# 38 more products on one tile of a fused attention and expert kernel

## The chip, the cores and the metric

The kernel runs on one core of a Trainium2 chip. The metric is the device time of one execution in microseconds. TensorE (PE) multiplies matrices, its weight loads are shown as PEld; VectorE (DVE), ScalarE (ACT) and GpSimd (POOL) work element by element, and SyncE (SP) issues most DMA transfers.

## The reference

Windowed causal attention over 8 batches, 8 heads, 576 positions and 64 channels per head, with a window of 64, followed by a gated expert layer (RMS norm, two products to 1536 columns, silu of one times the other, one product back to 512) over the 4608 tokens.

```python
scores = scale * np.matmul(q, k.transpose(0, 1, 3, 2))
mask = (rel >= 0) & (rel < window)
scores = np.where(mask, scores, -1000000000.0)
attn = np.exp(scores - np.max(scores, axis=-1, keepdims=True))
attn = attn / (np.sum(attn, axis=-1, keepdims=True) + 1e-09)
attn_out = np.matmul(attn, v)
x = np.ascontiguousarray(attn_out.transpose(0, 2, 1, 3)).reshape(B * S, H * D)
rms = np.sqrt(np.mean(x * x, axis=-1, keepdims=True) + 1e-06)
xn = x / rms * rms_g
g = xn @ w_gate
silu = g * (1.0 / (1.0 + np.exp(-g)))
val = xn @ w_val
out = silu * val @ w_out
```

The queries and keys are some four times larger than the draw that the reference's attention starts from, and the weights come as double precision.

## The kernel before, in words

Two heads make a pair; a batch has four pairs, so there are 32, and pair 4 is the first of the second batch. The expert layer takes the tokens in tiles of 512. The first batch's attention, the loading of the first weights and the first token tile are interleaved by hand: the program's steps are recorded, and then emitted in the order of the table ORDER. Each entry of it is an engine (t TensorE, v VectorE, s ScalarE, g GpSimd), the name of the tile that the step writes, and a count. Every engine takes its own steps in that order. Recorded steps are all listed under line 214, or 184 once recording is over.

The names that matter here:

- **ssq** holds the sums of squares of the first batch's attention output; tot adds them over partitions. VectorE then finds the inverse roots of the 576 means by a seed and three Newton steps, in ssq again.
- **rb** is the spread: four float32 products that copy the roots to all partitions (each shows as two passes in the profile).
- **xb** is the attention output, scaled by rb and the norm's weights; **xn** its two half-precision parts, high by ScalarE, low by GpSimd; **pv** and **pg** are the expert layer's first products, from xn.
- **mp** and **mn** are powers of two taken from the bytes of a double-precision weight, **pw** (bf16 products with a unit matrix) brings them together, and VectorE makes the float32 weight **wt** of it.
- **sc** are scores of a pair, **p** the masked scores, whose row minimum goes to st.
- **warm** are products of a constant with itself, which nothing reads. They are recorded as 24 tiles of up to 40 products; the table emits as many as it names.

TensorE writes into PSUM, which has eight banks. The pool ps_mi has one bank, and each tile that is taken from it is placed there:

```python
ps_mi = early.enter_context(tc.tile_pool(name="ps_mi", bufs=1, space=PSUM))
t = ps_mi.tile([P, TT], F32, tag="mi", name=f"warm_{k}")
n2 = ps_mi.tile([P, TT], F32, tag="mi", name=f"n2_{c}")[:, :2]
t = ps_mi.tile([P, TT], F32, tag="mi", name=f"sc_{n}_{g}_{h}")
```

The last of these is the scores of the second head of a pair from the second batch on (scores, line 630); the first head's are in ps_sc. VectorE reads the scores in the step masked. A tile framework adds the waits between engines, from what each instruction reads and writes and from which tiles share a place.

Of the kernel before, what the change touches and what calls it, by code (L numbers as in the profile page):

```python
# [90 lines left out]
g.ssq_0 s.mn_0_1 v.wt3 t.warm_1*2 t.tr_3_1_1*2 t.xp_3_0*6 v.top_0 t.xp_3_0*2 s.st_0_2 t.xp_3_0*2 t.pw_0_1_0 s.pt_3_1_1  # L91
t.pw_0_1_0 s.xb_0 s.kv_5 g.ssq_0 v.wt4 t.warm_1*2 t.xp_3_1*8 v.top_0 t.pw_0_1_1 s.xb_0 t.pw_0_1_1 s.kv_3 s.mp_1_1
v.sq_0 v.ssq_0 t.warm_1*3 t.n2_0 v.z_0 v.wt4 t.warm_2*2 t.tot_0*3 s.mn_1_1 t.tot_0 t.sc_4_0*3 v.ws_0 t.sc_4_0*2 v.wt3
t.sc_4_0 s.st_1_2 t.sc_4_0*4 s.kv_5 t.pw_1_1_0 v.ws_0 v.ssq_0 t.pw_1_1_0 v.ssq_0*2 s.mp_0_2 v.ssq_0*2 v.p_4_0_0
v.ssq_0*2 s.wt1 v.ssq_0*4 v.wt5 s.mn_0_2 t.rb_0_0 g.wt1 t.rb_0_0 v.p_4_0_1 t.rb_0_0 v.p_4_0_0 t.rb_0_0 v.p_4_0_0
t.pw_0_2_0 v.p_4_0_1 s.wt0 v.p_4_0_0 t.pw_0_2_0 v.xb_0 t.sc_4_1*2 v.wt6 t.sc_4_1 s.xn_0 t.sc_4_1*5 v.xb_0 t.pw_1_1_1
g.xn_0 t.pw_1_1_1 v.p_4_1_1 s.xn_0 v.xb_0 t.pv_0_0 s.mn_1_2 t.pv_0_0 g.xn_0 v.p_4_1_0 t.pv_0_0 v.wt5 t.pv_0_0 v.wt0
# [1428 lines left out]
```

## Time and profile before

| | us |
|---|---|
| Median of 3 runs (955.16 to 956.2) | 955.55 |
| The profiled execution | 954.38 |
| Its span, first to last instruction | 952.4 |
| TensorE busy | 931.9 |
| VectorE busy | 625.4 |
| ScalarE busy | 510.9 |
| GpSimd busy | 495.6 |

The page gives busy time by engine and in 40 slices, the chain of work that ended last, and groups of instructions by line, operation and tile. Beside it the trace answers for stretches of time (busy time of each engine, granted TensorE clock, DMA) and lists the instructions of an engine in order of time: start, length, engine, line, operation, output and inputs, count, and in brackets how long the engine sat idle before it and who ended that. The length of a TensorE product includes its way through the array, so products that follow each other overlap, and the distance of their starts is what one costs. The mean granted clock over the span is 0.996.

### The profile page before, as it was taken

How to read it: one execution, taken by the hardware profiler on the slowest of the kernel's cores; microseconds unless marked ns; L12 is line 12 of the kernel's file. 1: busy time of each engine (PE TensorE's matmuls, PEld its weight loads, DVE VectorE, ACT ScalarE, POOL GpSimd, SP SyncE). 2: the span in 40 equal slices, each digit the busy share in tenths (PEclk: the TensorE clock that was granted, in tenths of full speed). 3: DMA queues.
4: the chain of work that ended last, by engine and by line, in shares of the span. 5: the costliest groups of instructions: out<-in, count | busy, mean ns of one | idle time of the engine just before them, and what ended most of it. 6: DMA issues, size and time to landing. Idle time of an engine off the chain costs nothing.

```text
span 952.4 us, 20830 instructions
## 1 busy us (share of the span) xinstructions
PE 931.9 (98%) x7860; PEld 610.0 (64%) x7860; DVE 625.4 (66%) x1721; ACT 510.9 (54%) x1303; POOL 495.6 (52%) x634
## 2 busy tenths in 40 slices
PE   7699999999999999999999999999999999999998
PEld 5455454444454444788478856885688568848865
DVE  6888879778886876576757665776676555513540
ACT  7778985454444453566456645664465335413430
POOL 4355444978575783677466747764777122200210
PEclk9899999999999999999999999999999999999999
DMA  7655752515424661467245733564355226614300
GB/s 280 225 167 180 238 177 76 154 38 161 131 82 135 205 198 69 149 217 259 86 139 200 251 122 120 184 245 163 88 195 182 93 72 190 218 45 133 112 12 34
DMA packets 81316, 143.44 MB, mean 151 GB/s; under 512 B 25792, under 2 KB 38336, under 8 KB 81216
## 3 DMA queue, kind: packets, MB, share of 16 engines
q1 hardware_dynamic: 80640, 140.93, 45.4%
q8 instruction: 62, 1.02, 0.5%
q10 hardware_dynamic: 576, 1.18, 0.3%
q14 instruction: 38, 0.31, 0.1%
HBM read 121.64 MB, written 20.45 MB: 149 GB/s over the span
## 4 chain that ended last, share of the span: by engine, by line
PE 90%; DVE 3%; ACT 2%; POOL 2%; issue 1%; POOLq 0%; DVEq 0%; ACTq 0%
PE bk L184 51%; PE po L184 10%; PE pv L184 7%; PE pg L184 7%; PE xp L184 3%; PE pg L214 3%; PE pv L214 3%; PE sc L184 2%; POOL pm L184 1%; PE rb L184 1%; PE pw L214 1%; PE xp L214 1%; DVE ssq L214 1%; DVE th L184 1%; POOL h L184 0%
## 5 line engine op out<-in xcount | busy, mean ns | idle before, releaser
L184 PEld LDWEIGHTS <-wt 128*128 128x128 f16 x3624 | 353.2, 98 | 109.6 <-issue 4.6
L184 POOL TENSOR_TENSOR pm<-pm,st 32x288 f32<-32x288 f32 (+1 forms) x384 | 266.0, 693 | 62.4 <-DVE st L184 15.4
L184 PEld LDWEIGHTS <-h 128*128 128x128 f16 x1308 | 126.6, 98 | 142.3 <-issue 3.9
L184 PE MATMUL bk<-xn,wt 128*128 128x256 f16 x1728 | 207.3, 273 | 0.6 <-DVE u L184 0.5
L184 PE MATMUL bk<-wt,h 128*128 128x512 f16 (+1 forms) x900 | 191.1, 371 | 0.0
L184 POOL TENSOR_TENSOR h<-th,h 128x512 f16<-128x512 f32 x78 | 93.6, 1201 | 170.2 <-ACT h L184 156.2
L184 PE MATMUL bk<-wt,wt 128*128 128x256 f16 x1224 | 150.4, 273 | 0.3 <-ACT u L184 0.3
L184 ACT ACTIVATE pm<-pm,st 128x128 f32<-128x128 f32 (+1 forms) x216 | 83.9, 389 | 37.8 <-DVE st L184 36.7
L184 PE MATMUL po<-wt,h 128*128 128x512 f16 x408 | 90.9, 379 | 0.7 <-DVE wt L214 0.7
L184 ACT CAST h<-th 128x512 f16<-128x512 f32 x94 | 58.0, 617 | 51.7 <-DVE th L184 51.6
L184 POOL TENSOR_TENSOR xn<-xb,xn 128x448 f16<-128x448 f32 (+7 forms) x45 | 38.4, 861 | 83.5 <-ACT xn L184 81.1
L184 DVE SCALAR_TENSOR_TENSOR th<-th,bk 128x256 f32<-128x256 f32 x108 | 44.8, 415 | 49.6 <-ACT th L184 49.5
L184 ACT ACTIVATE th<-bk,hsc 128x256 f32<-128x256 f32 x108 | 48.0, 472 | 46.9 <-DVE bk L184 28.7
L184 DVE TENSOR_TENSOR bk<-bk,s 128x512 f32<-128x512 f32 x36 | 25.1, 696 | 69.2 <-PE bk L184 42.2
L184 PE MATMUL pv<-xn,wt 128*128 128x512 f16 x288 | 66.5, 379 | 0.0
L184 PE MATMUL pg<-xn,wt 128*128 128x512 f16 x288 | 66.1, 379 | 0.0
L184 ACT ACTIVATE ot<-bk,hsc 128x512 f32<-128x512 f32 (+1 forms) x25 | 16.8, 670 | 62.8 <-PE bk L184 62.8
L184 DVE CUSTOM_DVE_ANT_0 pm<-sc,blocked 128x128 f32<-128x128 f32 x191 | 48.7, 282 | 0.0
L184 DVE SCALAR_TENSOR_TENSOR th<-bk,th 128x256 f32<-128x256 f32 x108 | 45.8, 424 | 3.7
L214 PEld LDWEIGHTS <-wt 128*128 128x128 f16 x288 | 27.9, 99 | 31.6 <-issue 1.3
L184 ACT CAST xn<-xb 128x448 f16<-128x448 f32 (+7 forms) x56 | 23.8, 430 | 39.9 <-DVE xb L184 39.8
L184 DVE STREAM_TRANSPOSE pm<-pm 128x512 f32<-128x512 f32 (+1 forms) x72 | 39.6, 554 | 7.9 <-POOL pm L184 7.9
(179 smaller groups left out, 1318.2 us busy)
## 6 DMA issues: line engine op xcount, KB each, us to landing
wt<-sevens SPq DMA_DIRECT2D x108, 512.0 KB, 4.9
kv<-kv SPq DMA_DIRECT2D x28, 608.0 KB, 4.7
wt<-sevens SPq DMA_DIRECT2D x36, 256.0 KB, 3.1
q<-q SPq DMA_DIRECT2D x28, 288.0 KB, 3.7
kv<-kv SPq DMA_DIRECT2D x56, 128.0 KB, 5.0
out<-ot SPq DMA_DIRECT2D x27, 256.0 KB, 2.1
st<-w_gate SPq DMA_DIRECT2D x6, 1024.0 KB, 5.5
st<-w_val SPq DMA_DIRECT2D x6, 1024.0 KB, 5.3
```

What stands on the lines that cost most here:

```text
L184: return real(*args, **kw)
L214: steps[name].popleft()()
```

## The change

One entry is added to the table ORDER: 38 products of tile warm_3, each 128 by 128 by 256 columns in bf16.

```diff
-t.sc_4_0 s.st_1_2 t.sc_4_0*4 s.kv_5 t.pw_1_1_0 v.ws_0 v.ssq_0 t.pw_1_1_0 v.ssq_0*2 s.mp_0_2 v.ssq_0*2 v.p_4_0_0
+t.sc_4_0 s.st_1_2 t.sc_4_0*4 s.kv_5 t.pw_1_1_0 v.ws_0 v.ssq_0 t.pw_1_1_0 t.warm_3*38 v.ssq_0*2 s.mp_0_2 v.ssq_0*2 v.p_4_0_0
 v.ssq_0*2 s.wt1 v.ssq_0*4 v.wt5 s.mn_0_2 t.rb_0_0 g.wt1 t.rb_0_0 v.p_4_0_1 t.rb_0_0 v.p_4_0_0 t.rb_0_0 v.p_4_0_0
```

The products are those of keep_warm:

```python
for k in range(WARM[1]):
    t = ps_mi.tile([P, TT], F32, tag="mi", name=f"warm_{k}")
    for _ in range(WARM[0]):
        nc.tensor.matmul(t[:, :WC], lhsT=bright.to_broadcast([P, P]), rhs=bright.to_broadcast([P, WC]), start=True, stop=True)
```

On TensorE, before, from the last scores of pair 4's first half to the spread of the roots (the number behind a name is the buffer's, and in brackets stand the engines whose counters an instruction waits for):

```order
L214 MATMUL sc_4_0_1_270<-kv_4_265,q_4_264 64x64
L214 LDWEIGHTS unit_106 [waits DVE_49]
L214 MATMUL pw_1_1_0_276<-mp_1_1_274,unit_106 128x512 [waits Activation_49]
L214 LDWEIGHTS unit_106
L214 MATMUL pw_1_1_0_276<-mn_1_1_275,unit_106 128x512 [waits Activation_49]
L214 MATMUL rb_0_0_260<-ssq_0_185,first_of_108 128x144 [waits DVE_49,PE_49]
L214 MATMUL rb_0_0_260<-ssq_0_185,first_of_108 128x144 x2
L214 MATMUL rb_0_0_260<-ssq_0_185,first_of_108 128x80
```

The same place in the changed kernel, the first two of the 38 pairs and what follows the last:

```order
L214 MATMUL pw_1_1_0_276<-mn_1_1_275,unit_106 128x512 [waits Activation_49]
L214 LDWEIGHTS one_107 [waits DVE_49]
L214 MATMUL warm_3_137<-one_107 128x256 [waits PE_49]
L214 LDWEIGHTS one_107
L214 MATMUL warm_3_137<-one_107 128x256
...
L214 MATMUL rb_0_0_260<-ssq_0_185,first_of_108 128x144 x3
L214 MATMUL rb_0_0_260<-ssq_0_185,first_of_108 128x80
L214 LDWEIGHTS unit_106
```

Before, rb waited until VectorE's counter stood at 123, which its last Newton step sets. Now the first weight load of the block waits until it stands at 129, and rb has no wait of its own. On VectorE the rows of this place are the same in both kernels. The counter reaches 129 with the last row but one shown here, the read of the fifth mask:

```order
L214 SCALAR_TENSOR_TENSOR wt5_86<-st_1_1_259,pw_1_1_0_276 128x512 [waits DMAHW3_49,PE_49]
L214 ISA p_4_0_1_272,st_4_0_273<-sc_4_0_1_270,blocked_111 128x128
L214 ISA st_4_0_273 128x1
L214 ISA p_4_0_0_271,st_4_0_273<-sc_4_0_0_269,blocked_111 128x128
...
L214 ISA p_4_0_0_271,st_4_0_273<-sc_4_0_1_270,blocked_111 64x64
L214 ISA st_4_0_273 64x1
L214 SCALAR_TENSOR_TENSOR xb_0_184<-xb_0_184,gsb_114,rb_0_0_260 128x512 [waits PE_49]
```

Nothing moved on VectorE; TensorE's rb now stands behind the block.

## The prediction

> **What bounds the kernel now.** I read the page's head first, then the chain of waits, then the stretches of 2 us around the place of the change, and last the instructions of each engine there.
>
> ```profile
> span 952.4 us, 20830 instructions
> PE 931.9 (98%) x7860; PEld 610.0 (64%) x7860; DVE 625.4 (66%) x1721; ACT 510.9 (54%) x1303; POOL 495.6 (52%) x634
> PE 90%; DVE 3%; ACT 2%; POOL 2%; issue 1%; POOLq 0%; DVEq 0%; ACTq 0%
> 52.00:952.40 900.40, 894.82 (x7423) 586.06 (x7421) 584.44 (x1537) 472.32 (x1192) 473.25 (x595) 1.00 0.45 146
> ```
>
> TensorE is busy for 98% of the span and carries 90% of the chain that ended last. From 52 us to the end (the last row) it lacks 5.58 us of being busy throughout, at full clock (1.00). So whatever moves TensorE's work at 52 us moves the end by about as much. The change stands ahead of that point, in a stretch where TensorE does wait:
>
> ```profile
> core 0: us, PE busy (x) PEld busy (x) DVE busy (x) ACT busy (x) POOL busy (x), PEclk, DMA share, GB/s
> 38.00:40.00 2.00, 1.65 (x31) 0.85 (x30) 1.86 (x8) 2.00 (x2) 0.00 (x0) 1.00 0.98 306
> 40.00:42.00 2.00, 0.00 (x0) 0.00 (x0) 1.90 (x7) 2.00 (x3) 0.85 (x1) 0.95 0.89 329
> 42.00:44.00 2.00, 0.00 (x0) 0.00 (x0) 1.93 (x3) 1.23 (x2) 1.41 (x1) 0.50 0.61 220
> 44.00:46.00 2.00, 1.25 (x5) 1.29 (x6) 1.95 (x12) 0.00 (x0) 0.00 (x0) 0.50 0.00 0
> 46.00:48.00 2.00, 2.00 (x15) 1.16 (x17) 1.20 (x4) 0.31 (x1) 0.00 (x0) 0.50 0.01 4
> 48.00:50.00 2.00, 1.93 (x21) 0.88 (x14) 2.00 (x6) 1.17 (x3) 1.33 (x2) 0.84 0.00 0
> ```
>
> TensorE does nothing from 40 to 44 us, its granted clock (PEclk) falls to 0.50, and it is back at 1.00 only after 48 us. Finer stretches place both edges:
>
> ```profile
> 41.60:41.80 0.20, 0.00 (x0) 0.00 (x0) 0.20 (x1) 0.20 (x1) 0.20 (x1) 1.00 1.05 410
> 41.80:42.00 0.20, 0.00 (x0) 0.00 (x0) 0.20 (x1) 0.20 (x1) 0.20 (x1) 0.51 1.05 410
> 48.40:48.60 0.20, 0.20 (x8) 0.00 (x0) 0.20 (x2) 0.00 (x0) 0.20 (x1) 0.50 0.00 0
> 48.60:48.80 0.20, 0.20 (x5) 0.10 (x2) 0.20 (x1) 0.00 (x0) 0.20 (x1) 0.92 0.00 0
> ```
>
> The clock closes at 41.80. It opens at 48.63, because 0.92 is the mean of 0.03 us at 0.50 and 0.17 at 1.00. The instructions of TensorE in this stretch, and a few rows of the same view from elsewhere that price them (columns: start, length, engine, line, operation, out<-in, count; in brackets the idle time before and who ended it; the first row is the summary by tile, with the shortest, median and longest of 31 products in ns):
>
> ```profile
> L214 PE MATMUL warm<-one x31: 269/285/421, 0.9 to 37.8; 128*128 128x256 bf16 x31
> 0.90 3.17 PE L214 MATMUL warm<-one 128*128 128x256 bf16 x14 [0.90 <-DVE one L214]
> 6.36 0.62 PE L214 MATMUL warm<-one 128*128 128x256 bf16 x4
> 37.65 0.38 PE L214 MATMUL warm<-one 128*128 128x256 bf16 x2 [0.50 <-DVE z L214]
> 39.27 0.38 PE L214 MATMUL pw<-mn,unit 128*128 128x512 bf16 x1
> 44.74 2.12 PE L214 MATMUL rb<-ssq,first_of 128*128 128x144 f32 x8 [5.10 <-DVE ssq L214]
> 46.66 0.63 PE L214 MATMUL pw<-mp,unit 128*128 128x512 bf16 x1
> 47.09 0.63 PE L214 MATMUL pw<-mn,unit 128*128 128x512 bf16 x1
> 48.70 0.39 PE L214 MATMUL pw<-mp,unit 128*128 128x512 bf16 x1
> 48.93 0.38 PE L214 MATMUL pw<-mn,unit 128*128 128x512 bf16 x1
> 51.05 0.59 PE L214 MATMUL pv<-xn,wt 128*128 128x512 f16 x2 [0.65 <-POOL xn L214]
> 156.76 1.03 PE L184 MATMUL rb<-ssq,first_of 128*128 128x144 f32 x8
> ```
>
> TensorE's last work before the gap ends at 39.27 + 0.38 = 39.65. It then waits 5.10 us for VectorE's roots (ssq) and runs the spread, rb, at half clock in 2.12 us. What VectorE does meanwhile decides this case:
>
> ```profile
> 37.44 0.15 DVE L214 TENSOR_SCALAR z<-n 128x2 int32<-128x2 int32 x1
> 43.95 0.65 DVE L214 SCALAR_TENSOR_TENSOR ssq<-ssq 128x144 f32<-128x144 f32 x2
> 45.12 0.28 DVE L214 CUSTOM_DVE_ANT_0 p<-sc,blocked 128x128 f32<-128x128 f32 x1
> 46.13 0.08 DVE L214 DVE_READ_ACCUMULATOR2_ANT st<- 64x1 f32 x1
> 46.91 0.75 DVE L214 SCALAR_TENSOR_TENSOR xb<-xb,gsb,rb 128x512 f32<-128x512 f32 x1 [0.69 <-PE rb L214]
> 47.76 0.69 DVE L214 SCALAR_TENSOR_TENSOR wt<-st,pw 128x512 int32<-128x512 int32 x1
> 48.36 0.74 DVE L214 SCALAR_TENSOR_TENSOR xb<-xb,gsb,rb 128x512 f32<-128x512 f32 x1
> 49.14 0.62 ACT L214 CAST xn<-xb 128x512 f16<-128x512 f32 x1 [0.83 <-DVE xb L214]
> 49.83 1.17 POOL L214 TENSOR_TENSOR xn<-xb,xn 128x512 f16<-128x512 f32 x1 [0.29 <-ACT xn L214]
> ```
>
> The roots are ready at 44.60. From 45.12 to 46.21 VectorE masks the scores of pair 4, waiting for nothing, and then waits 0.69 us for rb. From there the stretch is a relay: xb, ScalarE's xn, GpSimd's xn, and TensorE's pv at 51.05.
>
> **The change part by part.** It adds 38 weight loads and 38 products on TensorE between pw_1_1_0 and rb_0_0, and nothing elsewhere. The order of VectorE, ScalarE, GpSimd and SyncE around it is the same. If the block could start at 39.65 it would fill the gap. But it can't: its output tile, warm_3, is in the only bank of pool ps_mi, and so is the tile sc_4_0_1, which TensorE has just written. The first weight load of the block carries a wait on VectorE, and the counter value in the built program is the one that the last mask read of pair 4 sets, the row that ends at 46.13 + 0.08 = 46.21. The trace has the like of it in small: the two warm products at 37.65 sat 0.50 us until VectorE had read n2, which lies in that bank (z in the row). So the block leaves the gap empty, and rb, which was free to start at 44.74, now queues behind 38 products that begin after 46.21. TensorE takes its work in the written order, so everything after rb queues too, and VectorE's xb, ScalarE's and GpSimd's xn with it. The masks themselves need only what TensorE wrote before 39.65, so there is no lock, and they stay where they are.
>
> *Start.* The wait on z ended at 37.44 + 0.15 and the products began 0.06 us later; rb began 0.14 us after the roots. I take 0.10: the block starts at 46.31.
>
> *Price of one product.* At half clock two pw products of 512 columns start 0.43 us apart (46.66, 47.09), so 0.215 us for 256 columns; at full clock 0.23 us (48.70, 48.93), so 0.11. The warm rows agree: one product takes 0.285 us from its start to its end (the summary's median), so 14 in 3.17 us are 0.22 apart, and 4 in 0.62 us 0.11. All at full clock would be 4.2 us, all at half 8.2.
>
> *When the clock opens.* TensorE stays idle 1.57 us longer than before, so the block starts at half clock. Before, work resumed at 44.74 and the clock opened at 48.63, 6.83 us after it closed; TensorE had been busy without a break over the last 3.41 us, half of that distance. If the clock is decided once each 3.41 us, the decision at 48.63 now sees a stretch in which TensorE worked for 2.3 of 3.41 us. Either that is enough, or the clock opens at 52.04. No row shows which: the 0.47 us of work from 44.74 to the decision that would have stood at 45.21 were not enough, 3.41 were. If the decisions do not stand at a fixed place in the program, the opening falls anywhere from 48.0 (half a stretch of work) to 53.1 (two whole stretches after 46.31).
>
> The Trainium skill says on this, in "TensorE: Matmul & The Clock Gate", Part 1, "What's actually happening", that the gate opens after one busy window of about 3.4 us, and that the window runs freely, so that the transition shifts with the phase in which the work meets it. The distance of 6.83 us in the rows above agrees with two such windows. By that rule alone the opening would fall between 49.7 and 53.1, and the sum would be +6.2 to +7.9 us.
>
> *Sum with the opening at 48.63.* Half clock for 48.63 - 46.31 = 2.32 us: 10.8 products. The other 27.2 at 0.11 take 2.99 us: rb starts at 51.62. At full clock rb takes half of 2.12, or a little under the 1.03 of the later one with four blocks of 144 columns: I take 1.00. xb follows 0.05 us later, as before: 52.67, against 46.91, +5.76. Behind it the two pw products now run at full clock, so that the next step of VectorE (wt) need not wait for them, and the second xb comes 1.33 instead of 1.45 us after the first (0.73 for xb and 0.60 for wt, against 46.91 to 48.36). That takes 0.1 off: +5.65 us for the second xb, and by the relay for pv, which starts at 56.70. ScalarE and GpSimd were waiting for the relay before (0.83 and 0.29 us), so they add nothing.
>
> *Sum with the opening at 52.04.* Each microsecond more at half clock does 4.65 products that would have taken 0.51 us, and so costs 0.49 us; 3.41 us cost 1.67: +7.3 us. At 48.0 it is +5.35, at 53.1 +7.85. I take the middle between the two decisions: +6.5.
>
> *What hides any of it.* After 52 us TensorE is the bound, and the waits in it that a late start could eat are few:
>
> ```profile
> PE po L184 <- DVE wt L214: 0.7, 1, 0.7
> PE bk L184 <- DVE u L184: 0.5, 2, 0.3
> PE obound L214 <- DVE omx L214: 0.4, 1, 0.4
> PE bk L184 <- ACT u L184: 0.3, 1, 0.3
> ```
>
> They are 1.9 us in all, and each is for an engine that follows TensorE's own results, so it moves along. I count nothing for them. Nothing is gained on the other side: the half clock of before cost the relay at most 0.7 us at xb, which is in the sum.
>
> The profiled execution took 954.38 us, the span of 952.4 and 2.0 around it. The three runs have a median of 955.55, so 1.17 more. Part of that may be a later opening of the clock in them, since some pv products behind 49 us would then run at half rate, which the changed kernel has no room for once its block has opened the clock. 954.38 + 6.5 = 960.9 if all of the difference is of that kind, 955.55 + 6.5 = 962.05 if none is. I predict 961.5 us.
>
> **The rivals.**
>
> *No wait, as the diff reads.* If the block ran from 39.65 it would end at 43.9, the clock would stay open, and rb would end near 45.75. xb could then start when the masks end, at 46.21 instead of 46.91: 0.7 us less, 0.8 with the pw pair. That is 954.75 us, not slower, and within the 0.2% (1.9 us) that a measurement of this kernel tells from no change. For it speaks the empty gap of 5.10 us; against it the shared bank, the wait in the built program and the warm row that waited for z.
>
> *The clock stays at half through the block.* 38 at 0.215 are 8.17 us, rb takes its 2.12: xb starts at 56.65, +9.7, or 965 us. For it: 2.3 us of work may not count, and every operand of the block is the same constant. Against it: the 14 warm products at the start take 0.22 us each, the 4 at 6.36 take 0.11, so such products did open the clock.
>
> *Part of it is swallowed.* If the four waits above and the relay vanished, some 2.5 us would go: +4, or 959.5 us. For it: only that ScalarE and GpSimd are little loaded there. Against it: the 5.58 us that TensorE lacks in 900.
>
> **How the numbers follow.** Forecast 0.86, no wait 0.06, half clock throughout 0.04, swallowed 0.04. The range takes the opening from 48.0 on the profiled time (959.7) to 53.1 on the median (963.4), widened by 0.2 at both ends for the start and rb: 959.5 to 963.6. Slower by over 0.2%: 0.94, the forecast and two rivals. Within 0.2%: 0.05, nearly all of the rival without the wait. Faster: 0.01, if that one brought over twice its sum.
>
> **What would show it.** In the changed profile the gap before the first warm product of the block is some 6.6 us, ended by VectorE's p or st, not 0. The block takes 4.7 to 7.5 us, its first products 0.215 apart and its last 0.11. rb takes about 1 us, VectorE waits 5 to 8 us before xb, and pv comes at 56.5 to 59. The granted clock is at 0.50 until 48 to 53. After that, distances in TensorE's work are as before. I would be wrong if the block starts near 39.7, if the clock in it never changes, or if TensorE's later waits shrink by over 1 us.

## The result, and the profile after

| | before | with the 38 products |
|---|---|---|
| Median, us | 955.36 | 961.27 |
| Lowest to highest of 6 runs | 953.94 to 956.2 | 959.95 to 962.12 |
| Span of the profiled execution | 952.4 | 959.5 |

The ratio is 1.0063, with a 95% interval of 1.005 to 1.0076: the change costs 5.9 us (4.8 to 7.3 by the interval). The prediction was 961.5 us, slower.

TensorE in the changed kernel in order of time, from the last product ahead of the block to the first products that the relay releases:

```profile
40.52 0.38 PE L214 MATMUL pw<-mn,unit 128*128 128x512 bf16 x1
47.52 5.79 PE L214 MATMUL warm<-one 128*128 128x256 bf16 x38 [6.62 <-DVE st L214]
53.15 1.08 PE L214 MATMUL rb<-ssq,first_of 128*128 128x144 f32 x8
54.06 0.38 PE L214 MATMUL pw<-mp,unit 128*128 128x512 bf16 x1
54.28 0.38 PE L214 MATMUL pw<-mn,unit 128*128 128x512 bf16 x1
58.21 0.59 PE L214 MATMUL pv<-xn,wt 128*128 128x512 f16 x2 [0.45 <-POOL xn L214]
```

The block sat 6.62 us until VectorE had written st, the row minima that the masks leave. VectorE's rows beside it:

```profile
45.20 0.65 DVE L214 SCALAR_TENSOR_TENSOR ssq<-ssq 128x144 f32<-128x144 f32 x2
47.38 0.08 DVE L214 DVE_READ_ACCUMULATOR2_ANT st<- 64x1 f32 x1
54.27 0.75 DVE L214 SCALAR_TENSOR_TENSOR xb<-xb,gsb,rb 128x512 f32<-128x512 f32 x1 [6.80 <-PE rb L214]
55.53 0.74 DVE L214 SCALAR_TENSOR_TENSOR xb<-xb,gsb,rb 128x512 f32<-128x512 f32 x1
```

The roots were ready at 45.85. The last mask ended at 47.46, the block began 0.06 us later, and VectorE then waited 6.80 us for rb, where it had waited 0.69.

The clock, in stretches of the same trace:

```profile
42.00:44.00 2.00, 0.00 (x0) 0.00 (x0) 1.90 (x6) 2.00 (x3) 1.28 (x1) 0.90 0.97 349
44.00:46.00 2.00, 0.00 (x0) 0.00 (x0) 1.93 (x4) 0.79 (x1) 1.00 (x1) 0.50 0.33 117
48.00:50.00 2.00, 2.00 (x11) 1.43 (x10) 0.00 (x0) 0.00 (x0) 0.00 (x0) 0.50 0.00 0
50.00:52.00 2.00, 2.00 (x18) 1.68 (x16) 0.00 (x0) 0.00 (x0) 0.00 (x0) 0.90 0.00 0
50.40:50.60 0.20, 0.20 (x4) 0.15 (x3) 0.00 (x0) 0.00 (x0) 0.00 (x0) 0.96 0.00 0
52.00:54.00 2.00, 2.00 (x20) 1.87 (x19) 0.00 (x0) 0.00 (x0) 0.00 (x0) 1.00 0.00 0
```

From 48 to 52 us no engine but TensorE does anything: the block is alone on the chain. In 2 us 11 products fall at half clock (48 to 50) and 18 where the clock opens (50 to 52); products that reach over an edge are counted on both sides. The clock closed at 43.59 (the row from 42 us has a mean of 0.90) and opened at 50.42 (the row from 50.40 has a mean of 0.96), which is 2.9 us after the block began.

Profiles start at different points, so I measure this stretch from one thing that the change cannot move: the start of the last pw product ahead of the gap (39.27 before, 40.52 here). From there to the pv that waits for GpSimd it is 51.05 - 39.27 = 11.78 us before, and 58.21 - 40.52 = 17.69 here: **+5.91 us**. The 1.25 us that the marker itself is later lie ahead of the change. With 5.91 they make 7.16 of the 7.1 us between the spans. Behind that point nothing is lost or gained: from this pv to the end of the span it is 901.35 us before (952.4 - 51.05) and 901.29 here (959.5 - 58.21). The chain of waits of the changed kernel has the block in it:

```profile
PE 91%; DVE 3%; ACT 2%; POOL 2%; issue 1%; DVEq 0%; POOLq 0%; ACTq 0%
PE bk L184 51%; PE po L184 10%; PE pv L184 7%; PE pg L184 6%; PE xp L184 3%; PE pg L214 3%; PE pv L214 3%; PE sc L184 2%; PE xp L214 1%; POOL pm L184 1%; PE rb L184 1%; PE tr L214 1%; PE warm L214 1%; PE pw L214 1%; DVE th L184 1%
```

PE warm has 1% of the span.

### The profile page after: what moved, and what is told of

The parts are those of the page before. It is cut to its first block, busy times and chain, and to the rows that moved or that the text cites. A ratio compares the mean times of both kernels' runs of the same rounds, so it can differ in the third digit from the quotient of the medians.

```text
span 959.5 us, 20892 instructions
## 1 busy us (share of the span) xinstructions
PE 937.9 (98%) x7887; PEld 615.2 (64%) x7898; DVE 625.6 (65%) x1721; ACT 511.0 (53%) x1303; POOL 495.7 (52%) x634
## 3 DMA queue, kind: packets, MB, share of 16 engines
q10 hardware_dynamic: 576, 1.18, 0.4%
## 4 chain that ended last, share of the span: by engine, by line
PE 91%; DVE 3%; ACT 2%; POOL 2%; issue 1%; DVEq 0%; POOLq 0%; ACTq 0%
PE bk L184 51%; PE po L184 10%; PE pv L184 7%; PE pg L184 6%; PE xp L184 3%; PE pg L214 3%; PE pv L214 3%; PE sc L184 2%; PE xp L214 1%; POOL pm L184 1%; PE rb L184 1%; PE tr L214 1%; PE warm L214 1%; PE pw L214 1%; DVE th L184 1%
```

## The experiments

The diffs are against the changed kernel, those of the filled start against the kernel before; of the long lines of the table they show only the part that differs.

**The same products in another bank.** The 38 products stand at the same place of TensorE's order, but write into rb's own tile, ahead of the spread itself.

```diff
-t.pw_1_1_0 t.warm_3*38 v.ssq_0*2
+t.pw_1_1_0 t.rb_0_0*38 v.ssq_0*2
         rb = x_bank(f"rb_{b}_{a}")
+        for _ in range(38 if b == a == 0 else 0):
+            nc.tensor.matmul(rb[:, :WC], lhsT=bright.to_broadcast([P, P]), rhs=bright.to_broadcast([P, WC]), start=True, stop=True)
```

> The same 38 products at the same place, written into the bank of rb, which VectorE has left at 39.3 us, instead of the bank that the scores of pair 4 hold. Theory (the wait for the masks makes the loss): the block starts as soon as pw_1_1_0 is through, takes 4.2 us, the granted clock stays at 1.00, rb starts when the roots are ready and takes 1.0 us instead of 2.1; xb starts when the masks end, and the time is 0.8 us under the kernel before, 954.6 us if that one takes 955.4. Rival (38 products on this path cost their 4.2 us or more wherever they write): 959.5 us or more.

Measured: 954.28 us against 955.35, ratio 0.9991 (0.9982 to 0.9999). TensorE and VectorE in order of time:

```profile
40.60 0.38 PE L214 MATMUL pw<-mn,unit 128*128 128x512 bf16 x1
40.82 4.42 PE L214 MATMUL rb<-one 128*128 128x256 bf16 x38
46.11 1.18 PE L214 MATMUL rb<-ssq,first_of 128*128 128x144 f32 x8 [0.87 <-DVE ssq L214]
51.65 0.59 PE L214 MATMUL pv<-xn,wt 128*128 128x512 f16 x2 [0.46 <-POOL xn L214]
47.59 0.08 DVE L214 DVE_READ_ACCUMULATOR2_ANT st<- 64x1 f32 x1
47.70 0.75 DVE L214 SCALAR_TENSOR_TENSOR xb<-xb,gsb,rb 128x512 f32<-128x512 f32 x1
```

and its clock:

```profile
42.00:44.00 2.00, 2.00 (x20) 1.77 (x19) 1.93 (x5) 2.00 (x3) 1.26 (x1) 1.00 1.03 388
44.00:46.00 2.00, 1.24 (x12) 0.85 (x9) 1.90 (x5) 0.80 (x1) 0.86 (x1) 1.00 0.31 107
46.00:48.00 2.00, 1.89 (x19) 1.47 (x23) 1.95 (x13) 0.00 (x0) 0.00 (x0) 1.00 0.02 4
```

The block starts without a wait, takes 4.42 us at full clock, and is through before the roots are. rb takes 1.18 us instead of 2.12 and is ready before the masks are, so xb follows the masks at once. From the marker to pv it is 11.05 us, 0.73 less than before. So the 38 products cost nothing at this place of TensorE's order; the bank they write to makes the whole difference between this kernel and the change, 7.0 us of the medians and 6.64 of the stretch.

**One product.** The bank of the scores, with one product instead of 38.

```diff
-t.pw_1_1_0 t.warm_3*38 v.ssq_0*2
+t.pw_1_1_0 t.warm_3 v.ssq_0*2
```

> One product of warm_3 instead of 38, in the bank of the scores: the wait with hardly any block behind it. Theory: the product starts at the end of the masks, rb 0.2 us behind it at half clock, so xb comes some 1.7 us later than before and the time is 1.6 us over the kernel before, 957.0 if that takes 955.4; so the wait alone is 1.6 of the 5.9 us and the products are the rest. Rival (the wait is free, since VectorE was behind anyway): 955.4. Other rival (the wait is nearly all): 960.5 or more.

Measured: 956.72 us, ratio 1.0017 (1.0008 to 1.0026), +1.4 us. TensorE:

```profile
38.73 0.38 PE L214 MATMUL pw<-mn,unit 128*128 128x512 bf16 x1
45.73 0.39 PE L214 MATMUL warm<-one 128*128 128x256 bf16 x1 [6.62 <-DVE st L214]
45.92 1.99 PE L214 MATMUL rb<-ssq,first_of 128*128 128x144 f32 x8
52.09 0.59 PE L214 MATMUL pv<-xn,wt 128*128 128x512 f16 x2 [0.64 <-POOL xn L214]
```

The wait is the same 6.62 us, and from the marker to pv it is 13.36, +1.58. That is what it costs to let rb wait for the masks and not for the roots, with 0.19 us for the one product in it (45.73 to 45.92). The other 4.3 of the 5.91 us come with the further 37 products.

**The masks first.** The change, but with VectorE's six masks of pair 4 behind the third of the eleven steps that make the roots; in the change one stands behind the fifth, and five behind the last.

```diff
-t.pw_1_1_0 t.warm_3*38 v.ssq_0*2 s.mp_0_2 v.ssq_0*2 v.p_4_0_0
-v.ssq_0*2 s.wt1 v.ssq_0*4 v.wt5 s.mn_0_2 t.rb_0_0 g.wt1 t.rb_0_0 v.p_4_0_1 t.rb_0_0 v.p_4_0_0 t.rb_0_0 v.p_4_0_0
-t.pw_0_2_0 v.p_4_0_1 s.wt0 v.p_4_0_0 t.pw_0_2_0
+t.pw_1_1_0 v.ssq_0*2 v.p_4_0_1 v.p_4_0_0 v.p_4_0_0 v.p_4_0_1 v.p_4_0_0 v.p_4_0_0 t.warm_3*38 s.mp_0_2 v.ssq_0*2
+v.ssq_0*2 s.wt1 v.ssq_0*4 v.wt5 s.mn_0_2 t.rb_0_0 g.wt1 t.rb_0_0 t.rb_0_0 t.rb_0_0
+t.pw_0_2_0 s.wt0 t.pw_0_2_0
```

> The 38 products in the bank of the scores as in the change, but VectorE masks the scores of pair 4 ahead of its last two Newton steps rather than after them. Theory: the block's wait ends some 2 us after pw_1_1_0 is through, the block fills what is left of the gap, and rb starts 0.1 us after the roots if the clock stays open (time as before, 955.3), or up to 2 us later if the clock closes in the shorter gap (up to 957.5). Rival (the block costs its length wherever VectorE masks): 960 us or more.

Measured: 954.68 us, ratio 0.9992 (0.9983 to 1.0001). TensorE, and two rows of VectorE:

```profile
39.87 0.38 PE L214 MATMUL pw<-mn,unit 128*128 128x512 bf16 x1
41.85 4.43 PE L214 MATMUL warm<-one 128*128 128x256 bf16 x38 [1.60 <-DVE st L214]
46.45 1.18 PE L214 MATMUL rb<-ssq,first_of 128*128 128x144 f32 x8 [0.17 <-DVE ssq L214]
51.62 0.59 PE L214 MATMUL pv<-xn,wt 128*128 128x512 f16 x2 [0.45 <-POOL xn L214]
45.75 0.65 DVE L214 SCALAR_TENSOR_TENSOR ssq<-ssq 128x144 f32<-128x144 f32 x2
47.67 0.75 DVE L214 SCALAR_TENSOR_TENSOR xb<-xb,gsb,rb 128x512 f32<-128x512 f32 x1 [0.55 <-PE rb L214]
```

The block still waits for st, but for 1.60 us, and it fits. The masks now stand ahead of the roots, so the roots are ready 6.53 us after the marker (46.40 - 39.87), where it was 5.33 (44.60 - 39.27). Of these 1.20 us rb, which now runs at full clock, gives back 0.94 (1.18 us against 2.12): xb is 0.16 later after the marker, and pv is not, with 11.75 us against 11.78. This kernel and the change have the same products in the same bank, behind the same readers; only when VectorE reads is different, and with it 5.9 us of the stretch and 6.6 of the medians. (The expectation speaks of the last two Newton steps; eight of the eleven steps, nearly three Newton steps, stand behind the masks.)

**Twice the block.**

```diff
-t.pw_1_1_0 t.warm_3*38 v.ssq_0*2
+t.pw_1_1_0 t.warm_3*38 t.warm_4*38 v.ssq_0*2
```

> 76 products instead of 38, the second half in a further tile of the same bank. Theory: the clock is open before the first 38 are through, so each of the further 38 costs 0.11 us: 4.2 us over the change, 965.4 us if that takes 961.3. Rival (the block runs at half clock to its end): 8.2 us over the change, 969.5 us.

Measured: 965.42 us, ratio 1.0106 (1.009 to 1.0123), 4.15 us over the change, or 0.11 for each of the further 38. TensorE, and the stretches that show the two prices and where the clock opens:

```profile
39.60 0.38 PE L214 MATMUL pw<-mn,unit 128*128 128x512 bf16 x1
46.70 11.16 PE L214 MATMUL warm<-one 128*128 128x256 bf16 x76 [6.72 <-DVE st L214]
62.76 0.59 PE L214 MATMUL pv<-xn,wt 128*128 128x512 f16 x2 [0.45 <-POOL xn L214]
44.00:46.00 2.00, 0.00 (x0) 0.00 (x0) 1.90 (x10) 0.00 (x0) 0.00 (x0) 0.66 0.01 3
46.00:48.00 2.00, 1.30 (x7) 0.93 (x8) 0.63 (x8) 0.00 (x0) 0.00 (x0) 0.50 0.02 4
48.00:50.00 2.00, 2.00 (x11) 1.44 (x10) 0.00 (x0) 0.00 (x0) 0.00 (x0) 0.50 0.00 0
50.00:52.00 2.00, 2.00 (x14) 1.50 (x13) 0.00 (x0) 0.00 (x0) 0.00 (x0) 0.63 0.00 0
56.00:58.00 2.00, 2.00 (x20) 1.81 (x19) 0.00 (x0) 0.00 (x0) 0.00 (x0) 1.00 0.00 0
44.64:48.06 3.42, 1.36 (x7) 0.99 (x8) 1.96 (x13) 0.00 (x0) 0.00 (x0) 0.50 0.01 2
```

Here the clock closed at 44.64, because 0.66 is the mean of 0.64 us at 1.00 and 1.36 at 0.50, and opened at 51.48, because 0.63 is the mean of 1.48 us at 0.50 and 0.52 at 1.00. The last row is the first half of that distance: 1.36 of 3.42 us of work did not open it.

The 4.15 us are a difference of medians, the one here of four runs from 964.7 to 966.85, and that it meets the expectation so closely is in part luck. In the profiled execution it is 62.76 - 39.60 = 23.16 us from the marker to pv, 5.47 more than in the change. The clock opened 4.78 us after the block's start there, 1.88 later than in the change, which at the prediction's 0.49 us for each microsecond is 0.92 of it; 38 at 0.11 are 4.2, the start is 0.1 later, and some 0.3 us are not explained. The rival, half clock to the end of the block, is out by the row from 56 us.

**A filled start.** The profiles had shown that the marker moves by over a microsecond, for a reason at the very start (below). The first of two kernels takes the block in rb's bank and 20 instead of 14 products at the program's start, the second only the latter.

```diff
-s.kv_3 t.warm_0*14 t.sc_0_0*8
+s.kv_3 t.warm_0*20 t.sc_0_0*8
```

> The 38 products in the bank of rb, and 20 instead of 14 warm products at the very start of the program, so that TensorE has no gap from 4.1 to 5.2 us. Theory (the runs differ by about 1.3 us because the clock opens at 5 us in some and at 9 to 11 us in others, by the phase in which the decisions fall): the scores of the first pair find the clock open or have it open 3 us sooner in most runs; 0.7 us less in the median than with 14, so 953.6 us and 1.8 us under the kernel before. Rival (the runs differ by when the first transfers land, not by the clock): no change against 14, 954.3 us, or slower where the added products hold up the first scores.

> The kernel before, without the 38 products, but with 20 instead of 14 warm products at the very start. Theory: the same 0.7 us, so 954.65 us against 955.35. Rival: 955.35.

Measured: 953.80 us against 955.05 with the block in rb's bank, ratio 0.9988 (0.9979 to 0.9998); 954.62 us without it, ratio 0.9996 (0.9987 to 1.0005). Both profiles have the first scores at the price of full clock, here the first of the two:

```profile
0.90 4.27 PE L214 MATMUL warm<-one 128*128 128x256 bf16 x20 [0.90 <-DVE one L214]
5.31 0.98 PE L214 MATMUL sc<-kv,q 64*64 64x128 f32 x22
```

But the second can't be told from the kernel before, and the first is under it by 1.25 us, where the block in rb's bank alone was under it by 1.07. So the expected 0.7 us are not shown: the longer start moved the median by 0.4 us without the block and by 0.2 with it, inside the intervals. The first of the two has the lowest median here, 0.12% under the kernel before, but it can't be told from the one without the longer start.

## Why the prediction was right

**The wait.** The prediction's first step was that the block would not start in the gap, because its bank holds the scores of pair 4. The block waited 6.62 us for VectorE (predicted 6.6); in another bank, at the same place, it did not wait; with one product it waited the same 6.62 us; with earlier masks 1.60 us. These runs leave the other readings no room: it is neither the products' place nor their number that puts them behind the masks, but who reads the bank last, and when.

**The sum.** It started 0.10 us after the masks by the prediction, and 0.06 in the trace. The price of one product, 0.215 and 0.11 us, was read off pw and held: 2.90 us at half clock are 13.5 products, the other 24.5 at 0.11 take 2.70, and these 5.60 us stand against 53.15 - 47.52 = 5.63 in the trace. The prediction gave +5.65 us at pv for an opening 2.32 us after the block's start, and 0.49 us for each microsecond more. The clock opened 2.9 us after it, so the formula says 5.65 + 0.58 x 0.49 = 5.93; the trace says 5.91. The run with one product separates the two parts: 1.58 us for the wait with one product, and the rest for the others.

**Luck in the number.** The forecast itself took +6.5 us, the middle of two openings, which is an opening some 4.0 us after the block's start. That was 0.6 us too much for this trace. It set the 6.5 on 954.96, the middle between the profiled execution and the median, and the median of six is 955.36, 0.4 more. The two errors nearly cancel, and so 961.5 is only 0.2 us over 961.27. That the medians differ by the trace's 5.91 to the last digit is chance too, with an interval from 4.8 to 7.3.

**The rival without the wait** was worked out as 0.8 us under the kernel before, and the run in rb's bank, in which it was made true, came out 1.07 under it, with 0.73 in the stretch itself. So the sum for this rival was right and its condition false, and what told them apart was small: the wait in the built program, and a row of two products that had sat 0.50 us for z in the same bank.

**Half clock through the block** was refuted by the change's own trace (0.96 at 50.4 us, 1.00 after), and **a part swallowed** by the span: 5.91 us at pv and 1.25 ahead of the gap are the whole of the 7.1, so nothing was swallowed.

**What was off.** The prediction put part of the 1.17 us between the profiled execution and the median of before down to a later opening of the clock near 49 us. The profiles point elsewhere, to the start. The first scores in the changed kernel, and then two stretches of it near 23 us:

```profile
5.21 1.75 PE L214 MATMUL sc<-kv,q 64*64 64x128 f32 x22 [1.13 <-DMA q<-q]
6.89 1.04 PE L214 MATMUL warm<-one 128*128 128x256 bf16 x4
19.71:23.12 3.41, 2.20 (x36) 1.55 (x35) 2.78 (x19) 3.06 (x13) 2.67 (x5) 1.00 0.88 300
23.12:26.53 3.41, 3.41 (x37) 2.58 (x34) 2.67 (x12) 3.41 (x14) 1.83 (x3) 0.50 1.04 401
```

Before, the 22 scores took 0.98 us and the 4 products 0.62. Here they take 1.75 and 1.04, the price of half clock, although the clock column has 1.00 there; its record seems to begin with the first change of the clock. Later the clock was at half from 23.12 to 26.53. The same 20 products of tile xp start at 20.18 before and at 20.95 here, so 0.77 of the marker's 1.25 us are there by then, and the rest comes with the second stretch, all in a part of the program that the change does not touch. In the kernel with the block in rb's bank the marker was as late (40.60) without that second stretch: its scores took the same 1.75 us, and 20 more from 9.69 still took 1.52, against 0.96 here. So executions can differ by a microsecond by where the clock's decisions fall in the first 30 us. Whether this is what parts the unprofiled runs from the profiled one isn't shown: they have no trace, and filling the start did not move the median clearly. For the forecast it weighed 0.6 us, since the prediction had taken the middle of the two readings.

## What to carry to other kernels

Work that only keeps TensorE busy is not free of dependencies: it writes somewhere, and whoever still has to read that place sets when it can start. Put it into a bank that is free then, here the one that the next product overwrites, and look at the first instruction's wait before counting on the gap. Since TensorE took its work in the written order, the filler went from cover to critical path once its start slipped by more than the gap could hold: 1.60 us of wait still fitted, 6.62 did not, and the block then ran at half clock first.

## What the runs showed of the hardware

The clock needed no fixed idle time to close, nor a full stretch of work to open. In the profiles shown it changed at distances of 3.41 us or twice that (23.12 to 26.53, 43.59 to 50.42, 44.64 to 51.48). It closed 2.15 us after TensorE's last work in the kernel before (41.80), 2.69 after it in the changed kernel (43.59 against 40.90), and 4.66 after it in the kernel with 76 products (44.64 against 39.98). At 23.12 in the changed kernel it closed after a stretch with 2.20 of 3.41 us of work, while in the kernel with 76 products a stretch with 2.00 (37.82 to 41.23, counted back from 44.64 in steps of 3.41) left it open; so the busy time of one stretch alone does not say when it closes. It opened at 50.42 after a stretch with 2.9 of 3.41 us of work, and not at 48.06 in the kernel with 76 products after one with 1.36 of 3.42.

The Trainium skill says in "TensorE: Matmul & The Clock Gate", Part 1, "What's actually happening", that the gate opens after a busy window of about 3.4 us and that the window runs freely. The distances and the shift from profile to profile agree with this; a window that was 85% busy was enough here, so the clock opened half a microsecond sooner than a whole window after the block's start (47.52 + 3.41 = 50.93).
